# Weights behind the first block's inputs, the second block's inputs in the weights' queue, and three blocks re-slotted

## The chip, the cores and the metric

One Trainium2 chip, of which the kernel uses one core. A core has five engines that run their own instruction streams: PE (TensorE, matrix multiply), DVE (VectorE), ACT (ScalarE), POOL (GpSimd) and SP (SyncE, which here only issues DMAs). The time is device microseconds of one execution; the time of a kernel is the median of several.

## The reference, cut to what matters

```python
# q, k, v, alpha: (4, 8, 768, 48) float32;  B, H, S, D
state = np.zeros((B, H, D, D))
for t in range(S):
    state = alpha[:, :, t, :, None] * state + np.einsum('bhd,bhe->bhde', k[:, :, t], v[:, :, t])
    y[:, :, t] = np.einsum('bhd,bhde->bhe', q[:, :, t], state)
x = y.transpose(0, 2, 1, 3).reshape(B * S, H * D)      # 3072 x 384
out = ((x @ w_a) * (x @ w_b)) @ w_out                  # w_a, w_b: 384 x 1536, w_out: 1536 x 384
```

A gated linear recurrence over 768 tokens for 32 heads, then a bilinear feed-forward over its 3072 output rows.

## The kernel before, in words

The sequence is cut into three stretches of 256 tokens, the batch into two pairs, which makes six blocks (`Chunk`, numbers 0 to 5, two batch rows `u` = 0, 1 and 256 tokens each). Blocks 0 and 1 are the first stretch of the two pairs and start from a zero state, blocks 2 and 3 the second, 4 and 5 the third. What is called the first block below is block 0, the second is block 1.

For each block the recurrence runs as a chain of steps. `ld` loads a (alpha), k, q and v; `L` takes logarithms on ACT and adds neighbours (`l2`); `A` forms running sums with one float32 matmul and exponentials of them on ACT (`beta`, `invb`); `mk`, `mq` multiply k and q with these (DVE); `C` transposes the results on PE (or `T` by a DMA) into `kqT`, copied out of PSUM by DVE or ACT; `D` multiplies queries with keys on PE and masks on DVE (`m`); `dec` brings the decay at each half's end to the partitions it scales, as `dec P` by 32 small matmuls (64 rows in the trace) and two exponentials, as `dec D` by two pairs of DMAs through DRAM (`row<-beta`, then `bl<-row`); `v` casts v to bfloat16 (`vx`); `K` updates the state (`Sm`, then `S`); `S`, `Y` and `G` put together the output `xT` of one `u`, which ACT or DVE copy out of PSUM.

The feed-forward of a block has 512 tokens: 12 slices `f` of w_a and w_b (two groups of three matmuls, 512 wide; ACT copies the first, DVE multiplies it with the second into `prod`), then 4 groups of 12 matmuls with w_out (`ff_o`), each followed by an ACT copy and two stores. `ff f u` is the same slice for one `u` only, 256 wide, so that a block's feed-forward can begin when one `u` is ready. `W lo hi` loads columns of w_a and w_b in eight DMAs, `Wo lo hi` four slices of w_out in one. `warm n` are n matmuls on a constant, `gate_w` and `gate_in` are one-element operations on POOL that wait for a load, or that a load must wait for.

Nothing here is scheduled by a compiler. `START` is a list in the order in which instructions are written out to all engines before block 0's feed-forward. From there `PLAN[c]` says at which of the 28 slots of block c's feed-forward (24 groups of three matmuls, then 4 of `ff_o`) which step of which block is written. A step's last letters name its engine or issuing queue: V = DVE, S = ACT, P = POOL, Y = SP. Each engine runs its instructions in that order and waits where an input is not there.

## Time and profile before

| | us |
|---|---|
| median of 3 runs (243.29 to 245.69) | 244.79 |
| the profiled execution | 244.95 |
| its span, first to last instruction | 243.2 |
| PE busy in the span | 205.0 (84%) |
| first feed-forward matmul of block 0 | 34.79 |
| `ff_o` of block 0 begins | 70.25 |
| `ff_o` of block 1 is over | 125.11 |

The span is what the profile shows; 1.75 us of the profiled execution lie around it. PE is the busiest engine, but its clock has two levels, 1.2 and 2.4 GHz, and the profile gives the granted share (0.50 or 1.00), so equal work may take twice as long in one stretch as in another.

### The profile page before, as it was taken

To read this page: it belongs to the slowest core of one execution; us is meant where nothing else is said; L and a number is where in the kernel's file an instruction comes from. 1 tells how busy PE (TensorE), PEld (TensorE's weight loads), DVE (VectorE), ACT (ScalarE), POOL (GpSimd) and SP (SyncE) were. 2 spreads that over 40 slices of the span, in tenths; PEclk is the share of its full clock that TensorE was granted. 3 is DMA by queue.
4 is the path that set the end of the run, shared out by engine and by line. 5 is a ranking of instruction groups with operands and counts; after the bars stand their busy time and mean duration, and the time that the engine had idled before them with its cause. 6 is when DMAs were issued, how large, how long until landed. Compare 5 with 4: busy or idle time off the path is not lost.

```text
span 243.2 us, 5797 instructions
## 1 busy us (share of the span) xinstructions
PE 205.0 (84%) x2458; PEld 118.8 (49%) x2486; DVE 127.7 (53%) x181; ACT 118.8 (49%) x201; POOL 46.8 (19%) x67
## 2 busy tenths in 40 slices
PE   7866137499999799099999999999999989999992
PEld 7654026345666355035654555545555455554461
DVE  6674213438662286068737894178941785125500
ACT  3820043866574777009437594368832424244420
POOL 8845100000508081081000902000000000000000
PEclk9965558959999999659999999999999999999999
DMA  7999999900185989609947497890087000140023
GB/s 179 247 195 178 158 198 256 214 3 3 35 229 122 321 210 261 129 13 268 182 84 153 107 262 156 165 141 3 2 140 157 12 0 3 32 97 3 0 51 79
DMA packets 45930, 30.69 MB, mean 126 GB/s; under 512 B 36673, under 2 KB 42065, under 8 KB 45905
## 3 DMA queue, kind: packets, MB, share of 16 engines
q1 hardware_dynamic: 39200, 14.21, 31.9%
q0 software_dynamic: 6704, 16.12, 29.2%
q8 instruction: 19, 0.31, 0.6%
q14 instruction: 7, 0.05, 0.1%
HBM read 25.98 MB, written 4.74 MB: 126 GB/s over the span
## 4 chain that ended last, share of the span: by engine, by line
PE 57%; DMA 18%; ACT 7%; issue 7%; SPq 4%; DVE 4%; POOL 1%; POOLq 0%; DVEq 0%; ACTq 0%
PE f L377 16%; PE f L358 15%; PE f L368 15%; DMA v_t<-in_v_dram 9%; DMA bl<-row 4%; SPq L169 3%; DMA k_t<-in_k_dram 3%; PE f L205 2%; DMA row<-beta 2%; PE s L279 2%; PE y L290 2%; PE y L306 1%; PE y L313 1%; ACT L183 1%; ACT vx L190 1%
## 5 line engine op out<-in xcount | busy, mean ns | idle before, releaser
L358 PE MATMUL f<-xT,wa_t 128*128 128x512 bf16 (+1 forms) x211 | 60.7, 381 | 3.5 <-ACT xT L297 1.3
L368 PE MATMUL f<-xT,wb_t 128*128 128x512 bf16 (+1 forms) x217 | 59.8, 377 | 0.8 <-issue 0.3
L377 PE MATMUL f<-wo_t,prod 128*128 128x384 bf16 x288 | 48.3, 326 | 0.0
L377 PEld LDWEIGHTS <-prod 128*128 128x128 bf16 x288 | 28.0, 98 | 19.2 <-issue 0.2
L280 DVE TENSOR_TENSOR m<-s,mask 128x1024 bf16<-128x1024 f32 x24 | 29.3, 1222 | 14.4 <-PE s L279 14.4
L358 PEld LDWEIGHTS <-wa_t 128*128 128x128 bf16 x228 | 21.4, 101 | 25.6 <-issue 6.1
L368 PEld LDWEIGHTS <-wb_t 128*128 128x128 bf16 x228 | 21.4, 100 | 22.6 <-issue 2.5
L379 ACT ACTIVATE ot<-f 128x384 f32<-128x384 f32 x24 | 11.7, 490 | 34.0 <-PE f L377 34.0
L205 PE MATMUL f<-l,ut_f 128*128 128x384 f32 x24 | 11.7, 574 | 4.3 <-DVE l L185 4.3
L297 ACT ACTIVATE xT<-y 128x256 bf16<-128x256 f32 (+1 forms) x18 | 10.3, 574 | 9.5 <-PE y L306 7.7
L279 PE MATMUL s<-kqT 64*64 64x128 bf16 x384 | 12.8, 239 | 1.5 <-DVE kqT L258 1.1
L290 PE MATMUL y<-kqT,Sm 64*64 64x128 bf16 x96 | 7.9, 240 | 6.7 <-POOL Sm L341 6.7
L213 DVE TENSOR_TENSOR QKp<-k_t,invb 128x768 bf16<-128x768 f32 x12 | 11.3, 952 | 2.5 <-DMA k_t<-in_k_dram 2.5
L206 DVE TENSOR_TENSOR le<-f,la 128x384 f32<-128x384 f32 x12 | 6.7, 556 | 10.9 <-PE f L205 10.9
L279 PEld LDWEIGHTS <-kqT 64*64 64x64 bf16 x384 | 8.8, 115 | 7.0 <-issue 4.0
L213 DVE TENSOR_TENSOR QKp<-q_t,beta 128x768 bf16<-128x768 f32 x12 | 11.4, 951 | 0.9 <-DMA q_t<-in_q_dram 0.9
L185 POOL TENSOR_TENSOR l<-la 128x768 f32<-128x768 f32 x3 | 5.4, 1812 | 30.0 <-ACT la L183 30.0
L183 ACT ACTIVATE la<-a_t 128x1536 f32<-128x1536 f32 (+1 forms) x7 | 9.1, 1300 | 3.1 <-DMA a_t<-in_alpha_dram 3.1
L327 PEld LDWEIGHTS <-QKp 64*64 64x64 bf16 x384 | 4.5, 114 | 11.7 <-issue 11.7
L290 PE MATMUL y<-kqT,S 64*64 64x128 bf16 x96 | 8.1, 242 | 2.2 <-DVE tmp L340 1.5
L290 PEld LDWEIGHTS <-Sm 64*64 64x64 bf16 x96 | 6.0, 121 | 6.9 <-POOL Sm L341 6.9
L252 PE MATMUL f<-ident,QKp 128*128 128x128 bf16 x96 | 8.1, 234 | 1.5 <-DVE QKp L213 1.5
(231 smaller groups left out, 278.7 us busy)
## 6 DMA issues: line engine op xcount, KB each, us to landing
out_dram<-ot SPq DMA_DIRECT2D x48, 96.0 KB, 2.2
a_t<-in_alpha_dram POOLq DMA_DIRECT2D x4, 768.0 KB, 9.8
q_t<-in_q_dram POOLq DMA_DIRECT2D x4, 768.0 KB, 7.7
k_t<-in_k_dram POOLq DMA_DIRECT2D x4, 768.0 KB, 11.0
v_t<-in_v_dram POOLq DMA_DIRECT2D x4, 768.0 KB, 8.9
wo_t<-in_moe_w_out_dram POOLq DMA_DIRECT2D x3, 384.0 KB, 14.4
a_t<-in_alpha_dram SPq DMA_DIRECT2D x2, 384.0 KB, 4.2
q_t<-in_q_dram SPq DMA_DIRECT2D x2, 384.0 KB, 5.6
```

The costliest lines, as they stand in the source:

```text
L183: nc.scalar.activation(out=ch.la[:, us].rearrange("p b h r d -> p (b h r d)"), in_=ch.a[:, us].rearrange("p b h r d -> p (b h r d)"), func ...
L205: nc.tensor.matmul(p, lhsT=ut_f32, rhs=ch.l2[:, u].rearrange("p h d -> p (h d)"), start=True, stop=True)
L213: eng.tensor_mul(dst[ch.c % 2][:, u, :, :, :D], src[:, u].rearrange("p h r d -> p r h d"), by[:, u])
L252: nc.tensor.transpose(t[:, j, r, p], src[:, u, r, hp:hp + 2, :].rearrange("s h d -> s (h d)"), ident)
L279: nc.tensor.matmul(s2[g * HC:(g + 1) * HC, r, p, rk, :], lhsT=keysT(ch, u, 2 * h + p, g, r, rk), rhs=queriesT(ch, u, 2 * h + p, g, rs), st ...
L280: nc.vector.tensor_mul(m.rearrange("p r a k s -> p (r a) (k s)"), s2.rearrange("p r a k s -> p (r a) (k s)"), maskn(4))
L290: nc.tensor.matmul(y[rs, g, p, :], lhsT=lhsT, rhs=queriesT(ch, u, p, g, rs), start=(p == 0), stop=False, skip_group_check=True)
L297: nc.scalar.activation(out=o_, in_=i_, func=AF.Copy)
L358: nc.tensor.matmul(ap, lhsT=wa_t[:, kk, f * 128:(f + 1) * 128], rhs=ff_x(ch, us)[:, kk], start=(kk == 0), stop=(kk == KT - 1))
L368: nc.tensor.matmul(bp, lhsT=wb_t[:, kk, f * 128:(f + 1) * 128], rhs=ff_x(ch, us)[:, kk], start=(kk == 0), stop=(kk == KT - 1))
L377: nc.tensor.matmul(op, lhsT=ch.prod[:, f, m * C:(m + 1) * C], rhs=wo_t[:, f, :], start=(f == 0), stop=(f == NFF - 1))
L379: nc.scalar.activation(out=ot, in_=op, func=AF.Copy)
```

## The change

Only the two tables change (and, since they are two lines longer, the numbers of all lines behind them, by 2). At the start, SP loads all eight half-inputs of block 0 (a, a, k, q, v, k, q, v), and nothing for block 1. POOL waits (`gate_w q 1`) for the second q of block 0, then issues all weights, in thirds, with a of block 1 ahead of the last third of w_a and w_b, and v, k, q, q, k, v of block 1 at the end. Fewer `warm` matmuls stand at the very start (18 for 52) and more between the steps of block 0. Block 1's steps stand in the last four slots (24 to 27) of block 0's feed-forward where they were spread over slots 0 to 26, and block 1 gets half-width slices (`ff f u`), as block 0 has. Block 2 takes its decay by matmuls (`dec P`) where it used DMAs (`dec D`), and its loads are written at slots 16 to 25 of block 0.

```diff
 START = [
-    (0, "new"), (0, "ld a 0 Y"), (0, "L 0 V"), (1, "new"), (0, "ld a 1 Y"), (0, "ld q 0 Y"), (1, "gate_in a 0"), (0, "ld k 0 Y"), (0, "ln"),
-    (0, "ld v 0 Y"), (0, "ld k 1 Y"), (0, "warm 52"), (0, "ld q 1 Y"), (0, "ld v 1 Y"), (0, "W 0 512"), (0, "L 1 V"), (0, "exp"), (1, "gate_in k 1"),
-    (0, "W 512 1536"), (1, "ld a * Y"), (0, "Wo 8 12"), (0, "A 0"), (0, "gate_w q 0"), (0, "Wo 0 4"), (0, "warm 22"), (0, "A 1"), (1, "ld q * Y"),
...
+    (0, "new"), (0, "ln"), (0, "ld a 0 Y"), (0, "ld a 1 Y"), (0, "ld k 0 Y"), (0, "L 0 V"), (0, "ld q 0 Y"), (0, "warm 18"), (0, "ld v 0 Y"),
+    (0, "ld k 1 Y"), (0, "ld q 1 Y"), (1, "new"), (0, "ld v 1 Y"), (0, "L 1 P"), (0, "A 0"), (0, "gate_w q 1"), (0, "W 0 512"), (0, "W 512 1024"),
+    (1, "ld a * P"), (0, "exp"), (0, "W 1024 1536"), (0, "Wo 4 8"), (0, "Wo 0 4"), (0, "A 1"), (1, "ld v 0 P"), (0, "Wo 8 12"), (1, "ld k 0 P"),
...
 PLAN = {
-    0: [(0, 1, "L * V"), (6, 1, "A 0"), (8, 1, "A 1"), (8, 1, "mk 0 V"), (9, 1, "mq 0 V"), (10, 1, "mk 1 V"), (11, 1, "dec P"), (14, 1, "mq 1 V"),
...
+    0: [(9, 1, "L * V"), (14, 1, "A 1"), (16, 1, "A 0"), (16, 1, "dec P"), (16, 2, "new"), (16, 2, "ld a * P"), (22, 2, "ld v * P"),
+        (24, 1, "v 0 S"), (25, 1, "mk 0 V"), (25, 2, "ld k * P"), (25, 2, "ld q * P"), (25, 1, "mq 0 V"), (25, 1, "C 0 0 V"), (25, 1, "C 0 1 S"),
...
-    1: [(1, 2, "mq 0 V"), (3, 3, "new"), (4, 3, "ld a * P"), (5, 2, "dec D"), (5, 2, "mq 1 V"), (5, 2, "mk 1 V"), (6, 2, "C 0 0 S"), (6, 2, "v * P"),
...
+    1: [(0, 1, "ff 1 1"), (2, 3, "new"), (5, 1, "ff 3 1"), (5, 3, "ld k * P"), (5, 3, "ld a * P"), (6, 1, "ff 2 1"), (6, 2, "L * V"),
+        (7, 3, "ld q * P"), (10, 1, "ff 0 1"), (10, 2, "A 0"), (10, 2, "A 1"), (11, 2, "mk 0 V"), (12, 2, "dec P"), (12, 3, "ld v * P"),
...
```

Place one, the loads. On SP, before: block 0's eight half-loads, then block 1's four whole ones (tiles a_t, q_t, k_t, v_t; 128x8x96 is a half-load, 128x16x96 a whole one).

```order
L169 DMA a_t<-in_alpha_dram 128x8x96 x2
L169 DMA q_t<-in_q_dram 128x8x96
L169 DMA k_t<-in_k_dram 128x8x96
L169 DMA v_t<-in_v_dram 128x8x96
L169 DMA k_t<-in_k_dram 128x8x96
L169 DMA q_t<-in_q_dram 128x8x96
L169 DMA v_t<-in_v_dram 128x8x96
L169 DMA a_t<-in_alpha_dram 128x16x96
L169 DMA q_t<-in_q_dram 128x16x96
L169 DMA k_t<-in_k_dram 128x16x96
L169 DMA v_t<-in_v_dram 128x16x96
```

After: block 0's alone, k ahead of q, and then the stores of block 0's output and of the first half of block 1's (ot).

```order
L171 DMA a_t<-in_alpha_dram 128x8x96 x2
L171 DMA k_t<-in_k_dram 128x8x96
L171 DMA q_t<-in_q_dram 128x8x96
L171 DMA v_t<-in_v_dram 128x8x96
L171 DMA k_t<-in_k_dram 128x8x96
L171 DMA q_t<-in_q_dram 128x8x96
L171 DMA v_t<-in_v_dram 128x8x96
L387 DMA out_dram<-ot 64x384 x12
```

Block 1's loads have left SP. On POOL, before, from the end of the weights' issue (wo_t; go is the gate's one-element tile; S_103 and tmp belong to the state update; the last two rows are loads of block 2):

```order
L149 DMA wo_t<-in_moe_w_out_dram 128x4x384
L401 COPY go<-q_t 1x1
L149 DMA wo_t<-in_moe_w_out_dram 128x4x384 x2
L341 TENSOR_TENSOR S_103<-tmp,bl_108 128x4x48
L341 TENSOR_TENSOR S_103<-tmp,bl_112 128x8x48
L169 DMA a_t<-in_alpha_dram 128x16x96
L169 DMA q_t<-in_q_dram 128x16x96
```

After, the same place, where the six half-loads at the end are block 1's:

```order
L151 DMA wo_t<-in_moe_w_out_dram 128x4x384 x2
L171 DMA v_t<-in_v_dram 128x8x96
L151 DMA wo_t<-in_moe_w_out_dram 128x4x384
L171 DMA k_t<-in_k_dram 128x8x96
L171 DMA q_t<-in_q_dram 128x8x96 x2
L171 DMA k_t<-in_k_dram 128x8x96
L171 DMA v_t<-in_v_dram 128x8x96
L343 TENSOR_TENSOR S_103<-tmp,bl_108 128x4x48
```

The rest of block 1's loads stand behind w_a, w_b and most of w_out, and the first state update of block 0 on POOL stands behind them.

Place two, the end of block 0's feed-forward on DVE. Before (rows with prod are block 0's products; kqT, Sm_105, tmp, m and xT are steps of block 1):

```order
L258 COPY kqT<-f 128x4x256
L337 TENSOR_TENSOR Sm_105<-s_838,bl_112 128x8x48
L340 TENSOR_TENSOR tmp<-s_838,Sm_105 128x384
L370 TENSOR_TENSOR prod<-as__836,f 128x512
L280 TENSOR_TENSOR m<-s_962,mask 128x1024
L370 TENSOR_TENSOR prod<-as__942,f 128x512
L280 TENSOR_TENSOR m<-s_993,mask 128x1024
L370 TENSOR_TENSOR prod<-as__990,f 128x512
L280 TENSOR_TENSOR m<-s_1027,mask 128x1024
L295 CAST xT<-y_944 128x2x3x128
L370 TENSOR_TENSOR prod<-as__1083,f 128x512
L280 TENSOR_TENSOR m<-s_1141,mask 128x1024
```

After:

```order
L372 TENSOR_TENSOR prod<-as__880,f 128x512
L215 TENSOR_TENSOR QKp_110<-k_t,invb 128x16x48
L215 TENSOR_TENSOR QKp_110<-q_t,beta 128x16x48
L260 COPY kqT<-f 128x4x256
L282 TENSOR_TENSOR m<-s_949,mask 128x1024
L339 TENSOR_TENSOR Sm_105<-y_967,bl_112 128x4x48
L342 TENSOR_TENSOR tmp<-y_967,Sm_105 128x192
L215 TENSOR_TENSOR QKp_110<-k_t,invb 128x16x48
L215 TENSOR_TENSOR QKp_110<-q_t,beta 128x16x48
L282 TENSOR_TENSOR m<-s_1041,mask 128x1024
L260 COPY kqT<-f 128x4x256 x2
L282 TENSOR_TENSOR m<-s_1140,mask 128x1024
```

The products come first, in one row, and block 1's steps from mk (QKp_110<-k_t) on stand behind the last product.

Place three, the decay of block 2 on SP. Before, behind the eight stores of block 0's output (row and bl_108 are block 2's decay):

```order
L385 DMA out_dram<-ot 64x384 x8
L219 DMA row<-beta 2x1x384 x2
L222 DMA bl_108<-row 48x16x1 x2
L262 DMA_TRANSPOSE kqT<-QKp_110 128x16x128
L385 DMA out_dram<-ot 64x384 x4
```

After, from the stores on:

```order
L387 DMA out_dram<-ot 64x384 x12
L264 DMA_TRANSPOSE kqT<-QKp_110 128x16x128
L387 DMA out_dram<-ot 64x384 x4
L221 DMA row<-beta 2x1x384 x2
L224 DMA bl_112<-row 48x16x1 x2
```

Block 2's pair of DMA steps is gone; the first pair left (bl_112) is block 3's.

## Rows read from the trace of the kernel before

**Rows 1.** The page, part 2: granted clock and DMA share in 40 slices of 6.08 us.

```profile
PEclk9965558959999999659999999999999999999999
DMA  7999999900185989609947497890087000140023
```

**Rows 2.** The waits: who waited for whom, total us, times, longest us.

```profile
ACT vx L190 <- DMA v_t<-in_v_dram: 10.7, 1, 10.7
PE y L327 <- ACT xT L297: 9.2, 1, 9.2
...
PE y L290 <- POOL Sm L341: 6.7, 1, 6.7
...
PE f L205 <- DVE l L185: 4.3, 2, 3.9
```

**Rows 3.** The timeline of SP: start us, us, then the issue.

```profile
5.77 1.44 SPq L169 DMA_DIRECT2D k_t<-in_k_dram  x1
...
13.67 19.94 SPq L169 DMA_DIRECT2D q_t<-in_q_dram  x1
```

**Rows 4.** The chain that ended last, in time: start us, us, what.

```profile
8.74 22.95 DMA v_t<-in_v_dram
31.72 0.84 ACT vx L190
...
33.47 0.71 ACT xT L297
...
56.00 0.83 PE s L234 x64
...
92.53 10.28 DMA bl<-row
...
104.81 1.40 PE f L358 x3
...
126.28 0.65 PE f L368 x3
...
148.01 7.80 PE f L377 x48
...
167.81 0.65 PE f L205 x2
...
178.16 7.80 PE f L377 x48
```

**Rows 5.** The timeline of PE: start us, us, line, operation, count [idle before it].

```profile
1.38 5.73 PE L201 MATMUL f<-ident 128*128 128x128 bf16 x52 [1.38 <-POOL ident masks.py:199]
...
12.70 1.07 PE L252 MATMUL f<-ident,QKp 128*128 128x128 bf16 x16 [1.23 <-DVE QKp L213]
...
22.50 1.06 PE L252 MATMUL f<-ident,QKp 128*128 128x128 bf16 x8
...
34.79 0.82 PE L358 MATMUL f<-xT,wa_t 128*128 128x256 bf16 x3
...
44.54 0.49 PE L368 MATMUL f<-xT,wb_t 128*128 128x256 bf16 x3
...
70.25 2.11 PE L377 MATMUL f<-wo_t,prod 128*128 128x384 bf16 x12
...
81.91 0.81 PE L358 MATMUL f<-xT,wa_t 128*128 128x512 bf16 x2 [0.36 <-ACT xT L297]
...
125.11 0.42 PE L279 MATMUL s<-kqT 64*64 64x128 bf16 x16
```

**Rows 6.** Two windows: length; busy PE, PEld, DVE, ACT, POOL; clock, DMA share, GB/s.

```profile
6.00:8.00 2.00, 1.61 (x13) 1.23 (x11) 1.79 (x3) 1.95 (x2) 2.00 (x6) 1.00 1.29 261
28.00:30.00 2.00, 0.00 (x0) 0.00 (x0) 0.00 (x0) 0.00 (x0) 0.00 (x0) 0.50 1.29 166
```

**Rows 7.** The tile wa_t: issue on POOL (ns min/median/max) and time to landing.

```profile
L145 POOL DMA_DIRECT2D wa_t<-in_moe_w_a_dram x4: 602/606/734, 6.7 to 14.9; - x4
...
DMA to landing us min/median/max: 6.5/7.9/10.8
```

**Rows 8.** The page, part 5: busy us, mean ns of one, idle before it.

```profile
L280 DVE TENSOR_TENSOR m<-s,mask 128x1024 bf16<-128x1024 f32 x24 | 29.3, 1222 | 14.4 <-PE s L279 14.4
...
L213 DVE TENSOR_TENSOR QKp<-q_t,beta 128x768 bf16<-128x768 f32 x12 | 11.4, 951 | 0.9 <-DMA q_t<-in_q_dram 0.9
```

46 rows, old and new, of tables (PLAN, START) are left out of this document.

## The prediction

> **What bounds the kernel now.** I read the clock and DMA lines of the page first, then the waits, the chain in order of time, and the timelines of SP and PE at the places that these name. The DMA engines are busy without a break for the first eight slices (48 us), and the clock falls to half in two early stretches and once more near 100 us [rows 1]. In the DMA-bound stretch PE stands still: 9.2 us before the state step L327, released by ACT, whose cast of v had waited 10.7 us for v's second half [rows 2]. That load was issued at 8.74 and took 22.95 us [rows 4], though the issues of the same size ahead of it took 1.44 us each [rows 3]. In between POOL's weights and block 1's loads had joined: SP's next loads crawl (one issue of 19.94 us [rows 3]) and the 261 GB/s of the inputs alone become 166 [rows 6]. So the first half-width feed-forward matmul comes at 34.79 [rows 5].
>
> Two more stops follow. After the half-width slices (the last group starts at 44.54 [rows 5]) the next work on PE is block 1's running sum, 3.9 us late [rows 2], and the clock goes with it [rows 1]. Then block 2's decay comes back through DRAM: 10.28 us for bl<-row, and PE waits 6.7 us before it can read Sm [rows 2, 4], after which three matmuls take 1.40 instead of 0.65 [rows 4]. Behind block 1's output, from 125.11 [rows 5], PE is hardly ever idle: the outputs of blocks 2 and 3 begin at 148.01 and 178.16 [rows 4], 30.15 us apart. That is the steady price of a block: 12 pairs of groups at 2 x 0.65 (15.6), four output groups (7.8), and 6.75 for the recurrence of one block that is transposed by DMA.
>
> **The loads after the change.** Block 0's inputs are 8 x 393 KB = 3.15 MB, alone on the DMA engines. At 261 GB/s [rows 6] from 2 us on they take 12 us: the second q lands near 12.6, the last v near 14. POOL waits for that q and issues the first weights then; with the 2 us or so that an issue needs to start moving data, weights flow from about 14.5. What do they cost? Block 0 and 1 inputs (6.29 MB) at 261 GB/s are 24 of the some 45 us that the DMA engines were busy without a break [rows 1], so the 3.54 MB of bfloat16 weights cost 21, or 7.1 us for each third, wo included. By that w_a and w_b's thirds land near 20, 25 and 34 (4.7 each, block 1's a of 3.0 between the last two), wo near 42, k and q of block 1's first row near 43 and 45, the last v near 49. The sum of the DMA work is unchanged, and so is its end; its order is what changes.
>
> **First feed-forward.** Had v been there, PE's last transposes (22.50 plus 1.06 [rows 5]) would have been followed by ACT's copy (0.9), its xT copy (0.71 [rows 4]) and the state step (0.6): 25.8, so 9.0 us of the 34.79 are v's. From the first transposes at 12.70 [rows 5] that is a chain of 13.1. Off it go 0.9 for the second q, which now is there [rows 8], and 0.7 for the xT copy, which moves to DVE ahead of the transposes. Against it stands the start: the 52 warming matmuls took 5.73 us [rows 5], 0.11 each, the price at 1.2 GHz. 18 of them end at 3.4, and nothing follows until the logarithms near 7.5. I take PE at the low level there: two sums at twice the 0.65 of [rows 4], 24 warming matmuls (2.6), dec P (0.83 [rows 4]): first transposes at 13.5 (12.0 if the clock holds, when DVE's products bound it). Together 13.5 + 13.1 - 1.6 = **25.0**. The weights it needs came near 20.
>
> **Rest of block 0.** Eight half-width pairs at 0.66, the output steps of the second row, and 2 us for a mask and a copy that they wait for: 9.2, against 10.1 in the rows (34.79 to 44.54 plus 0.3 [rows 5]); until 34.2. Eight full pairs at 1.30, block 1's two sums (1.3) and dec P (0.83) are 12.5; ACT must fit two table switches, the logarithm, eight exponentials and eight slice copies in the same stretch, which I price at 1.2: until 47.9 (`ff_o` stood at 70.25 [rows 5]). The stop of 3.9 goes, since a lands near 29 and its logarithm is wanted near 36. Two output groups end at 51.8.
>
> **Block 1's steps, now without cover.** They were spread over the feed-forward; now they stand in the last two output groups and behind them, and PE waits for DVE: mask 1.22 twice and products of 0.95 twice [rows 8] in a row are longer than the output group beside them. PE's own work is the lower bound: two output groups (3.9) and about 6 of steps, 9.9. The upper is what the same chain took in block 0, 13.1. I take 11.4, nearer the lower one because PE is at 2.4 GHz here: 63.2. Half-width slices with the second row's output steps between them: 6.6, until 69.8. This is the price of the change, some 5 us of PE idle that was not there.
>
> **Block 1's feed-forward.** The steady 30.15, less four pairs already done (5.2), plus block 2's transposes on PE and dec P (1.8 + 0.83) and block 3's two sums (1.3), is 28.9. Block 2's whole recurrence now falls on eight slices, not twelve, so ACT and DVE are as full as PE: 3 more (0, and 6 if every chain of block 2 is exposed as block 1's is). Block 1 is over at 101.7, against 125.11 [rows 5]; from its first full slice it used to take 43.2 us (81.91 to 125.11 [rows 5]). The decay's wait of 6.7 and the slow stretch behind it are gone with dec P.
>
> **Behind that** nothing of weight changes: as many steps of blocks 2 to 5, in nearly the same slots, on a PE that was busy anyway. 243.2 - 125.1 = 118.1, plus 0.3 for one D step of block 3 that moves behind the line. Span 220.1; with the 1.75 around it, 221.9 against the profiled 244.95, which is the median (244.79) within 0.1%. **Forecast: 222.0 us.**
>
> **Rivals.** *Late weights.* Before, weights moved from the first issue at 6.7 [rows 7] until about 40, 33 us for 3.54 MB, beside other traffic. If that is POOL's own pace, not sharing, wo lands at 14.5 + 33 + 4.5 (the inputs ahead of it) = 52.0 where I need it at 47.9, and the second q of the first pair comes about 1.5 too late as well: 227.5. Against: input loads on the same engines ran at 261 alone, and the mix at 166 [rows 6].
>
> *POOL is held while it issues.* 34 DMAs now go out on POOL while DVE works. If each waits for one DVE operation of some 0.69 us, the last v lands 23 us later, near 72, where block 1's second state step wants it near 59: 235. Against: the issues took 602 to 734 ns [rows 7] while DVE was busy 1.79 of 2 us [rows 6]. The Trainium skill (SBUF — State Buffer, Summary: rules for kernel authors) tells this way: descriptors of DMAs from GpSimd are starved while VectorE runs in its fast modes, and such DMAs should go out from another queue. By it, moving block 1's inputs to POOL is the wrong way; the durations in the trace do not show it.
>
> *Another wait for a decay.* Block 3's is now the first to go through DRAM, at the end of block 1. If it meets block 4's loads as block 2's met theirs (10.28 [rows 4]), PE waits 6.7 and loses about 2.8 to the low clock: 231.5. Against: block 4's loads are written seven slots and more ahead of it, as before.
>
> *The gate doesn't hold.* If weights still ran beside block 0's inputs, v would be late again and the first slice at 34.8: 231.8.
>
> *Slower: the clock stays low.* Between 25.0 and 101.7 lie 24 pairs and two blocks' outputs. At 1.2 GHz a pair takes 2.80 for 1.30 [rows 4] and an output twice as long: 24 x 1.5 + 15.6 = 52 us lost, 274. It decides from 23 us on, when under half of that work runs at 2.4 GHz. For it: the exposed chains of blocks 0 and 1 are full of short stops, and stops cost the clock before [rows 1]. Against: it came back within a slice each time that work resumed [rows 1], and warming matmuls fill the first chain.
>
> **How the numbers follow.** Forecast 0.66 (216 to 227: first slice 23.5 to 26.5, block 1's chain 9.9 to 13.1, crowding 0 to 6), late weights 0.15, decay 0.10, gate 0.03, POOL held 0.03, low clock 0.03. The range 212 to 234 leaves out the clock, POOL's hold, and the far ends of the others, since several of the terms could be off in the same direction. About 1% is what three runs of this kernel tell from no change (they span 2.4 us). Faster by over 1%: 0.94, all but the clock and combinations of several rivals; within 1%: 0.03; slower: 0.03.
>
> **What would show it.** First half-width slice near 25, not 35; the casts of v without a DMA wait; `ff_o` of block 0 near 48; block 1's output over near 102; no row<-beta before that; PE idle of some 5 us between 52 and 64; the last 118 us as before. Wrong if PE waits on wa_t, wb_t, wo_t or on block 1's k, q or v, or if the clock line shows half behind 30 us.

## The result, and the profile after

The changed kernel took 225.83 us (225.17 to 226.48, 4 runs) where the kernel before took 244.31 (243.29 to 245.69): a ratio of 0.924, with a 95% interval of 0.918 to 0.930. Forecast were 222.0 us and 212 to 234. The profiled execution took 226.01 us, its span 224.2. Medians below are over all executions; ratios leave out those in which the cores of a die ran longer at a lower clock (four of six in the repeat of the changed kernel, three of six with v on POOL, two of four with block 1's loads on SP, whose profile is of one, and one each without the gate and with the early decay).

The page, part 2: granted clock and DMA share in 40 slices, here of 5.6 us.

```profile
PEclk9999999999999988999999999999999999999998
DMA  7999999999999201999489995500782000320022
```

Against [rows 1] all three half-clock stretches are gone; a short one shows near 78 to 90 us (the record of the clock has it from 82.5 to 85.9). Of the stretch ahead of 10.8 us the record says nothing: its first row stands there, and the views print 1.00 where there is none. The DMA engines are busy without a break to 48.6 us in [rows 1] and to about 73 us here, since block 2's loads now follow at once (the first is issued at 41.7, before at 63.8).

The waits (who waited for whom, total us, times, longest us):

```profile
POOL wb_t L148 <- DMA a_t<-in_alpha_dram: 4.6, 1, 4.6
...
PE f L207 <- DVE l L187: 3.6, 1, 3.6
...
PE y L308 <- DVE m L282: 2.8, 3, 1.3
```

The three waits of PE in [rows 2] have no successor of their size; ACT's cast of v no longer waits for a load. The long waits for a load that are left are POOL's (the 4.6 here, and 5.6 at the gate); PE's longest, 3.6 us, is the start, where it waits for the first logarithms.

PE's timeline at the points that the prediction names (start us, us, line, operation, count, idle before it):

```profile
12.53 0.62 PE L254 MATMUL f<-ident,QKp 128*128 128x128 bf16 x8
...
21.96 0.49 PE L360 MATMUL f<-xT,wa_t 128*128 128x256 bf16 x3
...
30.80 0.81 PE L360 MATMUL f<-xT,wa_t 128*128 128x512 bf16 x2
...
44.98 4.06 PE L379 MATMUL f<-wo_t,prod 128*128 128x384 bf16 x24
...
61.10 0.50 PE L360 MATMUL f<-xT,wa_t 128*128 128x256 bf16 x3
...
67.26 0.81 PE L360 MATMUL f<-xT,wa_t 128*128 128x512 bf16 x2
...
102.99 0.81 PE L360 MATMUL f<-xT,wa_t 128*128 128x512 bf16 x2
```

The reader compares with [rows 5]: the first half-width slice came at 34.79 and comes at 21.96, 12.8 us earlier; `ff_o` of block 0 at 70.25 and now 44.98, 25.3 earlier, of which 12.8 are the first slice's and the rest comes of block 1's steps, with the stop of 3.9 among them, no longer standing between; block 1's output was over at 125.11 and is over at 102.99, 22.1 earlier. The span is 19.0 shorter. So 3.1 us of the lead are lost behind block 1. Most of that is at one place: the distance to block 2's output was 148.01 - 125.11 = 22.9 [rows 4, 5], and is now 128.21 - 102.99 = 25.2 (next fence).

The chain that ended last, around block 3's decay (start us, us, what):

```profile
107.27 1.66 DMA row<-beta
...
109.48 2.46 DMA bl<-row
...
112.06 0.57 DVE Sm L343
...
128.21 7.80 PE f L379 x48
...
158.79 7.80 PE f L379 x48
```

This is what [rows 4] showed of block 2's decay, in small: 2.46 us for bl<-row instead of 10.28, and PE idle 1.01 before it can read Sm and 1.20 before a mask's product.

### The profile page after: what moved, and what is told of

It reads as the page before. It is cut to its first block, busy times and chain, and to the rows that moved or that the text cites. A ratio compares the mean times of both kernels' runs of the same rounds, so it can differ in the third digit from the quotient of the medians.

```text
span 224.2 us, 6017 instructions
## 1 busy us (share of the span) xinstructions
PE 199.1 (89%) x2558; PEld 118.2 (53%) x2584; DVE 130.9 (58%) x189; ACT 120.2 (54%) x208; POOL 55.8 (25%) x79
## 4 chain that ended last, share of the span: by engine, by line
PE 74%; DVE 10%; issue 5%; ACT 5%; DMA 2%; POOL 1%; SPq 1%; POOLq 0%; DVEq 0%; ACTq 0%
PE f L379 21%; PE f L360 17%; PE f L370 17%; PE f L207 4%; DVE m L282 3%; PE s L281 3%; PE y L308 3%; PE y L292 2%; PE f L254 2%; PE y L315 1%; DVE kqT L260 1%; PE s L329 1%; DMA bl<-row 1%; PE f L203 1%; DVE mask L135 1%
## 5 line engine op out<-in xcount | busy, mean ns | idle before, releaser
L360 PE MATMUL f<-xT,wa_t 128*128 128x512 bf16 (+1 forms) x229 | 59.1, 358 | 2.6 <-ACT as__760 L364 1.3
L370 PE MATMUL f<-xT,wb_t 128*128 128x512 bf16 (+1 forms) x225 | 58.7, 359 | 2.4 <-ACT as__1368 L364 1.2
L360 PEld LDWEIGHTS <-wa_t 128*128 128x128 bf16 x240 | 22.4, 98 | 22.6 <-issue 2.7
L370 PEld LDWEIGHTS <-wb_t 128*128 128x128 bf16 x240 | 22.1, 98 | 22.4 <-issue 3.1
L381 ACT ACTIVATE ot<-f 128x384 f32<-128x384 f32 x24 | 11.8, 491 | 35.0 <-PE f L379 34.9
L187 POOL TENSOR_TENSOR l<-la 128x768 f32<-128x768 f32 (+1 forms) x3 | 4.6, 1534 | 43.7 <-ACT la L185 43.6
L281 PE MATMUL s<-kqT 64*64 64x128 bf16 x384 | 11.4, 221 | 1.4 <-DVE kqT L260 0.7
L342 DVE TENSOR_TENSOR tmp<-s,S 128x384 f32<-128x384 f32 x4 | 2.2, 558 | 15.9 <-PE s L329 15.9
L281 PEld LDWEIGHTS <-kqT 64*64 64x64 bf16 x384 | 7.7, 105 | 6.0 <-issue 3.9
L308 PE MATMUL y<-m,vx 64*48 64x128 bf16 x384 | 7.6, 217 | 2.8 <-DVE m L282 2.8
L258 ACT ACTIVATE kqT<-f 128x1024 bf16<-128x1024 bf16 x5 | 5.1, 1023 | 8.9 <-PE f L254 8.8
L308 PEld LDWEIGHTS <-vx 64*48 64x48 bf16 x384 | 6.0, 99 | 5.9 <-issue 5.8
L292 PE MATMUL y<-kqT,S 64*64 64x128 bf16 x96 | 7.0, 221 | 2.3 <-DVE tmp L342 1.5
```

The costliest lines, as they stand in the source:

```text
L281: nc.tensor.matmul(s2[g * HC:(g + 1) * HC, r, p, rk, :], lhsT=keysT(ch, u, 2 * h + p, g, r, rk), rhs=queriesT(ch, u, 2 * h + p, g, rs), st ...
L292: nc.tensor.matmul(y[rs, g, p, :], lhsT=lhsT, rhs=queriesT(ch, u, p, g, rs), start=(p == 0), stop=False, skip_group_check=True)
L308: nc.tensor.matmul(ch.y[u][r * DP:r * DP + D, g, p, :], lhsT=ch.vx[g * HC:(g + 1) * HC, u, 2 * p + r, rk, :], rhs=ch.m[u, p // 2][g * HC:( ...
L360: nc.tensor.matmul(ap, lhsT=wa_t[:, kk, f * 128:(f + 1) * 128], rhs=ff_x(ch, us)[:, kk], start=(kk == 0), stop=(kk == KT - 1))
L370: nc.tensor.matmul(bp, lhsT=wb_t[:, kk, f * 128:(f + 1) * 128], rhs=ff_x(ch, us)[:, kk], start=(kk == 0), stop=(kk == KT - 1))
L381: nc.scalar.activation(out=ot, in_=op, func=AF.Copy)
```

## The experiments

All start from the changed kernel unless another is named. Differences between variants of it under some 1.5% can't be told apart by the times (executions of one variant spread over up to 3.3 us), so there the milestones of the profile decide.

**The loads alone.** The order of the kernel before, with the new order and queues of the loads.

```diff
-    (0, "new"), (0, "ld a 0 Y"), (0, "L 0 V"), (1, "new"), (0, "ld a 1 Y"), (0, "ld q 0 Y"), (1, "gate_in a 0"), (0, "ld k 0 Y"), (0, "ln"),
-    (0, "ld v 0 Y"), (0, "ld k 1 Y"), (0, "warm 52"), (0, "ld q 1 Y"), (0, "ld v 1 Y"), (0, "W 0 512"), (0, "L 1 V"), (0, "exp"), (1, "gate_in k 1"),
-    (0, "W 512 1536"), (1, "ld a * Y"), (0, "Wo 8 12"), (0, "A 0"), (0, "gate_w q 0"), (0, "Wo 0 4"), (0, "warm 22"), (0, "A 1"), (1, "ld q * Y"),
-    (0, "dec P"), (1, "ld k * Y"), (0, "warm 4"), (0, "Wo 4 8"), (0, "mq 0 V"), (0, "mk 0 V"), (0, "C 0 0 V"), (0, "C 0 1 S"), (0, "v 0 V"),
-    (0, "D 0 0 s2"), (0, "K 0 V y2"), (1, "ld v * Y"), (0, "mk 1 V"), (0, "S 0"), (0, "D 0 1 s2"), (0, "mq 1 V"), (0, "Y 0 S"), (0, "v 1 S"),
+    (0, "new"), (0, "ld a 0 Y"), (0, "L 0 V"), (1, "new"), (0, "ld a 1 Y"), (0, "ld k 0 Y"), (0, "ld q 0 Y"), (0, "ln"),
+    (0, "ld v 0 Y"), (0, "ld k 1 Y"), (0, "warm 52"), (0, "ld q 1 Y"), (0, "ld v 1 Y"),
+    (0, "gate_w q 1"), (0, "W 0 512"), (0, "W 512 1024"), (1, "ld a * P"), (0, "W 1024 1536"), (0, "Wo 4 8"), (0, "Wo 0 4"), (1, "ld v 0 P"), (0, "Wo 8 12"),
+    (1, "ld k 0 P"), (1, "ld q 0 P"), (1, "ld q 1 P"), (1, "ld k 1 P"), (1, "ld v 1 P"),
+    (0, "L 1 V"), (0, "exp"), (0, "A 0"), (0, "warm 22"), (0, "A 1"),
...
```

> The kernel before with the loads, the gate and the weights of the changed kernel, in its order and on its queues; all other steps of START and all slots of the plan as before (steps of block 1 spread over block 0's slots, no half-width slices for block 1, block 2's decay by DMA). If order alone makes the gain: 226 us. If the slots make it: 244 us. Mine: the first half-width slice comes near 23 as in the changed kernel, but block 1's steps in the middle of block 0's slots then wait for k, q and v that land near 45 to 50, and block 2's decay still waits: 232 to 237 us.

Measured: 240.16 us, ratio 0.989 (0.984 to 0.994). PE's timeline:

```profile
24.75 0.82 PE L360 MATMUL f<-xT,wa_t 128*128 128x256 bf16 x3
...
39.14 1.65 PE L207 MATMUL f<-l,ut_f 128*128 128x384 f32 x2 [3.93 <-DVE l L187]
...
53.32 0.81 PE L360 MATMUL f<-xT,wa_t 128*128 128x512 bf16 x3 [2.73 <-DVE prod L372]
...
77.07 0.81 PE L360 MATMUL f<-xT,wa_t 128*128 128x512 bf16 x2 [0.36 <-ACT xT L299]
...
99.90 0.32 PE L292 MATMUL y<-kqT,Sm 64*64 64x128 bf16 x2 [7.38 <-POOL Sm L343]
```

The first slice is 10.0 us earlier than in [rows 5], as the loads promise. Of that, 4.8 are left at block 1's first full slice (81.91 in [rows 5], 77.07 here): the stop of 3.9 for block 1's running sum has only moved with the rest, though its input lay there from 33.8 on (in these slots it hangs on the order of the steps, not on the load), and block 1's v, now the last load of all, holds ACT for 2.93 and with it PE. At 99.90 the wait for block 2's decay is there again, even longer. The loads alone bring 1.1%. The other half, the new slots on the old loads, was not run.

**The loads, and block 2's decay by matmuls.**

```diff
-    1: [(1, 2, "mq 0 V"), (3, 3, "new"), (4, 3, "ld a * P"), (5, 2, "dec D"), (5, 2, "mq 1 V"), (5, 2, "mk 1 V"), (6, 2, "C 0 0 S"), (6, 2, "v * P"),
+    1: [(1, 2, "mq 0 V"), (3, 3, "new"), (4, 3, "ld a * P"), (5, 2, "dec P"), (5, 2, "mq 1 V"), (5, 2, "mk 1 V"), (6, 2, "C 0 0 S"), (6, 2, "v * P"),
```

> The order of the kernel before, with the new order of the loads, and block 2's decay by matmuls in place of DMAs (same slot). With the loads alone it took 240.2, with PE waiting 7.4 for block 2's Sm at 99.9 and three slices at half clock behind it. If that wait ate the gain of the loads, it is gone here: 240.2 - 7.4 - 2.0 (clock) + 0.8 (64 small matmuls) = 231.6, range 230 to 234, and block 2's outputs begin some 8 us earlier. Rival: the old slots, with block 1's steps waiting for block 1's own loads (a, then v), set the time and the decay only stood in their shadow: 238 to 240.

Measured: 231.56 us, ratio 0.949 (0.945 to 0.953), as expected. By the ratios the step from "dec D" to "dec P" is worth 4.0%, some 9.7 us (8.6 by the medians, which were taken on two chips), and the output of block 2 begins at 134.07 instead of 142.89, 8.8 earlier. The wait for one small transfer, with the half-clock stretch behind it, cost nearly what the loads had gained at the first slice.

**Block 2's decay back to DMAs, in the changed kernel.**

```diff
-        (7, 3, "ld q * P"), (10, 1, "ff 0 1"), (10, 2, "A 0"), (10, 2, "A 1"), (11, 2, "mk 0 V"), (12, 2, "dec P"), (12, 3, "ld v * P"),
+        (7, 3, "ld q * P"), (10, 1, "ff 0 1"), (10, 2, "A 0"), (10, 2, "A 1"), (11, 2, "mk 0 V"), (12, 2, "dec D"), (12, 3, "ld v * P"),
```

> The changed kernel with block 2's decay through DRAM again (dec D for dec P in slot 12 of block 1), as before. If dec P itself took the stop of 6.7 us and the slow clock behind it away: those 9 us come back, 235 us. Mine: in the changed kernel no load is on its way between 75 and 89 us, so the two DMA steps take some 2 us each, end ahead of the state step that wants them, and PE is spared 0.8 us of small matmuls: 225 to 226 us. That would say that it was the meeting with the loads, not the way through DRAM, that cost the time.

Measured: 226.00 us, ratio 0.930 (0.924 to 0.937); its profile's span is 223.7. No difference that can be told. SP's timeline:

```profile
75.90 1.32 SPq L221 DMA_DIRECT2D row<-beta  x2
78.45 0.92 SPq L224 DMA_DIRECT2D bl<-row  x2
```

The same transfers, in a lull of the DMA engines (2, 0 and 1 tenths from 73 to 90 us in the line above), hold nobody: the second bl<-row has landed at 81.1, 2.7 us after the first was issued, and the state update that reads it starts at 84.2. So it was not the way through DRAM that cost 9 to 10 us, but the moment, with 3.1 us to spare where 10.28 would not have fitted: with the slots placed anew the decay could have stayed as it was.

**Without the gate.** `gate_w q 1` left out, so that POOL issues weights from 7.96 on.

```diff
-    (0, "ld k 1 Y"), (0, "ld q 1 Y"), (1, "new"), (0, "ld v 1 Y"), (0, "L 1 P"), (0, "A 0"), (0, "gate_w q 1"), (0, "W 0 512"), (0, "W 512 1024"),
+    (0, "ld k 1 Y"), (0, "ld q 1 Y"), (1, "new"), (0, "ld v 1 Y"), (0, "L 1 P"), (0, "A 0"), (0, "W 0 512"), (0, "W 512 1024"),
```

> The changed kernel with only the gate taken out, so that POOL issues the weights some 5 us earlier, beside block 0's k, q and v; every byte and every other step as in the changed kernel. Order theory (the weights' packets beside block 0's inputs are what made v late): the second half of v lands well after 20 us instead of near 15, the first half-width slice comes near 32 instead of 21.96, and about 8 to 10 us are lost: 234 us. Rival (the gain comes from the new slots, and earlier weights only help): 225 to 226 us.

Measured: 231.74 us, ratio 0.951 (0.944 to 0.958): the gate is worth 2.7%, but not by the way that was expected. ACT's timeline, and then PE's:

```profile
22.44 0.84 ACT L192 ACTIVATE vx<-v_t 128x768 bf16<-128x768 f32 x1 [7.30 <-DMA v_t<-in_v_dram]
```

```profile
19.33 0.36 PE L281 MATMUL s<-kqT 64*64 64x128 bf16 x12 [2.15 <-issue]
...
24.34 0.50 PE L360 MATMUL f<-xT,wa_t 128*128 128x256 bf16 x3
...
117.39 0.31 PE L292 MATMUL y<-kqT,Sm 64*64 64x128 bf16 x2 [3.56 <-DVE Sm L343]
```

v waits again, but lands at 22.4, not at 31.7 as in [rows 4], because POOL itself stood for 4.9 us in seven stops between its issues (each until an earlier weight DMA had landed), and block 1's loads are not on SP. But it is not v that makes the first slice 2.4 late. PE had already lost 2.15 us from 17.18 on, in the middle of a group of like matmuls and with nothing to wait for ("issue"), and all that follows comes 2.4 later at the changed kernel's distances; v's cast was over at 23.28, and the state step that needs it began at 23.96, 0.55 behind the transposes ahead of it, as in the changed kernel. By itself v would have held that step by at most 1.8 (an estimate: 23.28 against 21.48 in the changed kernel).

What PE stood for is a reading, not an experiment. The trace holds packets of 16 KB that carry instructions (the page, part 3, has 20 of them on its queue q8). One is on its way here from 16.46 to 17.85, and PE goes on 1.48 behind its end; in the changed kernel one took from 13.95 to 15.10, and PE did not stand. So PE's own instructions seem to have come late beside weights and inputs.

Of the lead lost, 2.2 us are still left at block 1's last two output groups (101.25, against 99.09). The other 2.4 of the 4.6 by which its span is longer come later, at block 3's decay. The chain there:

```profile
112.01 4.12 DMA bl<-row
```

Where it took 2.46 in the changed kernel it takes 4.12, and PE waits 3.56 for Sm. This belongs to coming 2 us late, not to the gate: the repeat of the changed kernel below, whose profiled execution is 2.15 late at block 1's last two output groups for another reason (half clock from 61.1 to 64.5), shows 4.27 for bl<-row and the same 3.56 on PE. What makes the transfer longer there was not tried.

**Block 1's loads on SP.** They follow block 0's there and run beside the weights.

```diff
-    (1, "ld a * P"), (0, "exp"), (0, "W 1024 1536"), (0, "Wo 4 8"), (0, "Wo 0 4"), (0, "A 1"), (1, "ld v 0 P"), (0, "Wo 8 12"), (1, "ld k 0 P"),
-    (1, "ld q 0 P"), (1, "ld q 1 P"), (0, "warm 24"), (1, "ld k 1 P"), (1, "ld v 1 P"), (0, "mk 0 V"), (0, "dec P"), (0, "v 0 S"), (0, "mq 0 V"),
+    (1, "ld a * Y"), (0, "exp"), (0, "W 1024 1536"), (0, "Wo 4 8"), (0, "Wo 0 4"), (0, "A 1"), (1, "ld v 0 Y"), (0, "Wo 8 12"), (1, "ld k 0 Y"),
+    (1, "ld q 0 Y"), (1, "ld q 1 Y"), (0, "warm 24"), (1, "ld k 1 Y"), (1, "ld v 1 Y"), (0, "mk 0 V"), (0, "dec P"), (0, "v 0 S"), (0, "mq 0 V"),
```

> The changed kernel with block 1's loads issued on SP behind block 0's, where nothing holds them, instead of on POOL between and behind the weights. Order theory: they now run beside the weights and take their turns, so the first third of the weights lands near 26 instead of 20 and the later thirds and wo later too, while block 1's inputs come earlier than they are needed: PE waits 4 to 6 us, 230 to 232 us. Rival (the DMA engines do the same sum of work, and which queue issues it does not matter): 226 us. A third, the skill's rule that POOL's issue is starved beside VectorE: faster than the changed kernel, 223 us or less.

Measured: 234.66 us, ratio 0.956 (0.947 to 0.966). The tile wa_t, time from issue to landing, first here and then in the changed kernel:

```profile
DMA to landing us min/median/max: 6.6/7.4/8.1
```

```profile
DMA to landing us min/median/max: 3.0/4.2/8.6
```

The weights take 7.4 us where they took 4.2, and the first slice comes at 27.68, 5.7 late. But PE waits for no weight here. It stands twice ahead of that slice, both times in the middle of a group of like matmuls and with no releaser, 4.9 us together:

```profile
19.61 0.36 PE L281 MATMUL s<-kqT 64*64 64x128 bf16 x12 [2.13 <-issue]
...
27.45 0.24 PE L329 MATMUL y<-vx,QKp 64*64 64x48 bf16 x4 [2.77 <-issue]
```

The first stop is at PE's 449th instruction, the same one as without the gate, the second 256 instructions on. The packets of instructions take from 16.92 to 18.11 and from 24.54 to 25.83, where the changed kernel has them at 13.95 to 15.10 and 19.32 to 20.22; PE goes on 1.50 and 1.62 behind their ends. The granted clock is 1.00 in the record from 11.8 to 28.9, so neither stop is the clock's doing. So moving the loads cost 3.2% by the ratios, some 7.9 us, and at the first slice the loss is in these stops. That they come of the loads beside them is read from two runs that agree, and was not tried by itself. What the slower weights would have cost can't be told from this run.

**Without the warming matmuls between the steps** (24, 6, 8, 14 and 18 of them left out).

```diff
-    (1, "ld q 0 P"), (1, "ld q 1 P"), (0, "warm 24"), (1, "ld k 1 P"), (1, "ld v 1 P"), (0, "mk 0 V"), (0, "dec P"), (0, "v 0 S"), (0, "mq 0 V"),
-    (0, "C 0 0 V"), (0, "warm 6"), (0, "C 0 1 S"), (0, "D 0 0 s2"), (0, "K 0 P y2"), (0, "warm 8"), (0, "warm 14"), (0, "v 1 S"), (0, "S 0"),
-    (0, "mk 1 V"), (0, "D 0 1 s2"), (0, "mq 1 V"), (0, "warm 18"), (0, "Y 0 V"), (0, "C 1 0 V"), (0, "G 0 V"), (0, "D 1 0 s2"), (0, "C 1 1 S"),
+    (1, "ld q 0 P"), (1, "ld q 1 P"), (1, "ld k 1 P"), (1, "ld v 1 P"), (0, "mk 0 V"), (0, "dec P"), (0, "v 0 S"), (0, "mq 0 V"),
+    (0, "C 0 0 V"), (0, "C 0 1 S"), (0, "D 0 0 s2"), (0, "K 0 P y2"), (0, "v 1 S"), (0, "S 0"),
+    (0, "mk 1 V"), (0, "D 0 1 s2"), (0, "mq 1 V"), (0, "Y 0 V"), (0, "C 1 0 V"), (0, "G 0 V"), (0, "D 1 0 s2"), (0, "C 1 1 S"),
```

> The changed kernel without the 70 warming matmuls between block 0's steps (24, 6, 8, 14 and 18); the 18 at the start stay. If they hold the clock: the granted clock shows half from about 10 to 25 us, the transposes, sums and half-width slices take twice as long there, and 2 to 4 us are lost: 228 to 230 us. Rival (PE waits for DVE there anyway, so that nothing is lost but idle time): 225.5 to 226.5 us.

Measured: 229.52 us, ratio 0.943 (0.938 to 0.948). PE's timeline:

```profile
19.24 1.05 PE L308 MATMUL y<-m,vx 64*48 64x128 bf16 x32 [1.33 <-DVE m L282]
20.23 1.04 PE L254 MATMUL f<-ident,QKp 128*128 128x128 bf16 x8
...
24.16 0.60 PE L360 MATMUL f<-xT,wa_t 128*128 128x256 bf16 x3
```

And a window of it (length; busy PE, PEld, DVE, ACT, POOL; clock, DMA share, GB/s):

```profile
20.00:24.00 4.00, 3.86 (x82) 3.04 (x73) 3.18 (x5) 0.31 (x1) 3.63 (x6) 1.00 1.18 180
```

The same y<-m,vx took 0.63 in the changed kernel, the same transposes 0.70 and 0.62. PE ran its chain at the lower level: 1.04 for eight such transposes is the 1.06 of [rows 5], from a half-clock stretch. The 1.00 in the window is no record of the clock: in this run its first row stands at 24.39 us, and the views print 1.00 where there is none. First slice 2.2 late: the 70 small matmuls pay for themselves before the feed-forward begins.

**Block 3's decay earlier**, from slot 27 to 24 of block 1's feed-forward, and so ahead of its transposing DMAs on SP.

```diff
-        (21, 3, "mk 0 V"), (22, 3, "A 1"), (22, 2, "S 1"), (22, 2, "D 1 1 s2"), (23, 3, "mk 1 V"), (24, 2, "Y 1 S"), (25, 2, "G 1 S"),
-        (25, 3, "mq 0 V"), (25, 3, "T 0 Y"), (26, 3, "mq 1 V"), (27, 3, "dec D"), (27, 3, "T 1 Y"), (27, 4, "ld a * P")],
+        (21, 3, "mk 0 V"), (22, 3, "A 1"), (22, 2, "S 1"), (22, 2, "D 1 1 s2"), (23, 3, "mk 1 V"), (24, 2, "Y 1 S"), (24, 3, "dec D"), (25, 2, "G 1 S"),
+        (25, 3, "mq 0 V"), (25, 3, "T 0 Y"), (26, 3, "mq 1 V"), (27, 3, "T 1 Y"), (27, 4, "ld a * P")],
```

> The changed kernel with block 3's decay (by DMA) written in slot 24 of block 1 instead of slot 27. In the changed kernel its first DMA stands on SP behind the stores of block 1's output, is issued at 106.5 though its input is there at 95.9, and its result lands at 111.9, where DVE and then PE wait for it (2.4 us idle on PE, and more behind). Theory: it is SP's order; issued behind the first store, it lands ahead of need, 2.5 to 3.5 us gained: 222.5 to 223.5 us. Rival (the wait is DVE's full list, the DMA only ends last by a little; DVE waited 0.7 us for it): 225 to 226 us.

Measured: 228.48 us, ratio 0.938 (0.933 to 0.943); a gain is excluded. SP's timeline, and then PE's:

```profile
98.51 1.31 SPq L221 DMA_DIRECT2D row<-beta  x2
103.42 0.91 SPq L224 DMA_DIRECT2D bl<-row  x2
...
105.71 2.12 SPq L264 DMA_TRANSPOSE kqT<-QKp  x1
```

```profile
110.22 0.42 PE L281 MATMUL s<-kqT 64*64 64x128 bf16 x16 [2.02 <-DMA kqT<-QKp]
```

SP, having issued row<-beta, stands from 99.82 until 103.42 for its return, and the transposing DMA behind it goes out 4.95 later than in the changed kernel (105.71 for 100.76). PE now waits 2.02 for kqT and 0.46 for Sm. The wait has changed its name.

**Block 3's decay by matmuls.**

```diff
-        (25, 3, "mq 0 V"), (25, 3, "T 0 Y"), (26, 3, "mq 1 V"), (27, 3, "dec D"), (27, 3, "T 1 Y"), (27, 4, "ld a * P")],
+        (25, 3, "mq 0 V"), (25, 3, "T 0 Y"), (26, 3, "mq 1 V"), (27, 3, "dec P"), (27, 3, "T 1 Y"), (27, 4, "ld a * P")],
```

> The changed kernel with block 3's decay by matmuls in place of DMAs. PE stood about 2.2 us in all between 110.9 and 116.4 behind a row<-beta that SP could issue only at 106.5, behind block 1's stores, and a bl that landed at 111.9. My theory: that is the last wait for a decay; without it 2.2 less 0.8 for the small matmuls: 224.4 by the run of 225.8 (1.0 to 1.8 below the repeat of the changed kernel beside it), with no idle over 0.5 us on PE in front of the y matmuls of block 3. Rival: PE waits as long for the masks and for S next (DVE is full there) and pays the matmuls on top: 226 to 227.

Measured: 228.97 us, ratio 0.936 (0.931 to 0.940), span 224.5 in the profile: no gain. At its place the expected happened; further on stands another wait. PE's timeline:

```profile
112.69 0.24 PE L292 MATMUL y<-kqT,Sm 64*64 64x128 bf16 x2 [0.34 <-DVE Sm L343]
...
126.79 7.96 PE L379 MATMUL f<-wo_t,prod 128*128 128x384 bf16 x48
...
140.39 0.81 PE L370 MATMUL f<-xT,wb_t 128*128 128x512 bf16 x3 [1.64 <-DVE prod L372]
```

And DVE's, just ahead of the last of these:

```profile
139.18 0.56 DVE L343 TENSOR_TENSOR Sm<-tmp,bl 128x384 bf16<-128x384 f32 x1 [2.51 <-DMA bl<-row]
```

Block 2's output begins 1.3 us earlier (126.79 for 128.05 in the same view of the changed kernel). Then DVE stands 2.51 in front of block 4's Sm, whose decay also goes through DRAM, a product queues behind it, and PE loses 1.64. In the changed kernel DVE came to the same instruction at 138.10 and found the decay there. With block 4's decay by matmuls too, the lead might hold; that was not tried.

**Block 3's logarithm later**, from slot 15 to 19 of block 1's feed-forward, its sum on DVE.

```diff
-        (15, 3, "L * P"), (16, 2, "D 0 0 s2"), (16, 2, "K * P"), (17, 2, "C 1 1 S"), (18, 2, "S 0"), (18, 4, "new"), (18, 2, "D 0 1 s2"),
+        (16, 2, "D 0 0 s2"), (16, 2, "K * P"), (17, 2, "C 1 1 S"), (18, 2, "S 0"), (18, 4, "new"), (18, 2, "D 0 1 s2"), (19, 3, "L * V"),
```

> The changed kernel with block 3's logarithm and neighbour sum written at slot 19 of block 1 (and the sum on DVE) where they stood at slot 15. ACT worked without a break from 67.1 to 83.1, and the last piece of that was this logarithm (2.8 us with its table load); PE stood 1.33 at 82.4 and the clock was at half until 85.5. If ACT's load in that stretch is what block 1's feed-forward pays for, its output is over 1.5 to 2.5 us earlier (about 101 for 103.0), the clock stays at full level, and the time is 224 (1.5 to 2 below the repeat). Rival: the work only moves to where block 2's xT copies and the exponentials of block 3 stand; 226 to 228 and a stop of PE near 90 instead.

Measured: 228.23 us, ratio 0.936 (0.932 to 0.939). Two windows of it (columns as above):

```profile
79.00:82.00 3.00, 1.40 (x35) 0.61 (x36) 2.70 (x4) 0.95 (x2) 0.00 (x0) 1.00 0.00 0
82.00:86.00 4.00, 4.00 (x78) 2.14 (x75) 1.71 (x3) 1.02 (x1) 1.91 (x3) 0.57 0.01 4
```

And PE's timeline:

```profile
81.89 0.78 PE L329 MATMUL s<-vx,QKp 64*64 64x48 bf16 x64 [1.33 <-DVE m L282]
90.55 0.91 PE L207 MATMUL f<-l,ut_f 128*128 128x384 f32 x2 [1.48 <-DVE l L187]
```

ACT is free (0.95 busy of 3, it was 2.97), and the stop of 1.33 and the low clock are there all the same. My theory, ACT's load, falls. Another stop of 1.48 has come to it.

**Block 2's cast of v on POOL**, instead of ACT.

```diff
-        (12, 2, "mq 0 V"), (13, 2, "mk 1 V"), (13, 2, "mq 1 V"), (14, 2, "C 0 0 V"), (14, 2, "v * S"), (15, 2, "C 0 1 S"), (15, 2, "C 1 0 V"),
+        (12, 2, "mq 0 V"), (13, 2, "mk 1 V"), (13, 2, "mq 1 V"), (14, 2, "C 0 0 V"), (14, 2, "v * P"), (15, 2, "C 0 1 S"), (15, 2, "C 1 0 V"),
```

> The changed kernel with block 2's cast of v on POOL, idle there, instead of ACT. In the changed kernel ACT works without a break from 67.5 to 83 us, and the cast (1.48 us) stands ahead of the copy of the transposes that PE's next slice and the next mask wait for. If ACT's list sets the pace in block 1's crowded slots: 1 to 1.5 us gained, 224.5 us. If DVE's does (its products end only 0.4 us ahead of that copy): no change within 0.5 us.

Measured: 228.63 us, ratio 0.928 (0.922 to 0.934); not told from the changed kernel. Its profile has the best span of all, 223.3, with the stop in front of block 2's K there (1.53) and the clock behind it held.

**Both, the earlier decay of block 3 and v on POOL** (the diffs of these two together).

> Both of the last two together: block 3's decay in slot 24 and block 2's cast of v on POOL. If the two losses are separate, the gains add: 221.5 to 222.5 us. If one hides the other, no better than the better of the two.

Measured: 227.25 us, ratio 0.932 (0.928 to 0.936). PE waits 1.86 for the transposing DMA, as with the early decay alone.

**The changed kernel once more**, beside the last three.

> The changed kernel once more, on the chip of these three: the measure for differences of one per cent. 225.8, between 225 and 228; milestones within 0.7 of the first profile (first half-width slice 22.0, output of block 0 begins 45.0, first half-width slice of block 1 61.1, output of block 1 over 103.0).

Measured: ratio 0.926 (0.920 to 0.931), from executions of 225.60 and 226.31 us. None of the six variants of its slots is shown to beat it; the early decay, the decay by matmuls and the later logarithm are 1.0 to 1.5% slower by the ratios, close to what can be told.

## Why the prediction was right, point by point

The forecast was 3.8 us too low, by terms that erred to both sides. By the steps of the prediction, with the measured pieces from the timeline of PE above:

| step | predicted us | measured us |
|---|---|---|
| first half-width slice | 25.0 | 21.96 |
| half-width slices of block 0 | 9.2 | 8.84 |
| to `ff_o` of block 0 | 13.7 | 14.18 |
| two output groups and block 1's chain | 15.3 | 16.12 |
| block 1's half-width slices | 6.6 | 6.16 |
| to the end of block 1's output | 31.9 | 35.73 |
| the rest | 118.4 | 121.21 |
| span | 220.1 | 224.2 |

**The loads** went as worked out in their order, somewhat late: the gate at 13.54 for 12.6, block 1's a at 32.8 for 29 (ACT's logarithm starts then, and PE stands 1.34 us at 36.2 in its wake), the last v of block 1 at 52.3 for 49. POOL's timeline:

```profile
13.54 0.18 POOL L403 COPY go<-q_t 1x1 f32<-1x1 f32 x1 [5.63 <-DMA q_t<-in_q_dram]
13.66 0.74 POOL L147 DMA_DIRECT2D wa_t<-in_moe_w_a_dram  x1
...
33.08 0.53 POOL L148 DMA_DIRECT2D wb_t<-in_moe_w_b_dram  x1 [4.57 <-DMA a_t<-in_alpha_dram]
```

**First slice, 3.0 too late in the forecast.** The chain from the first transposes was taken from the kernel before, where PE ran it at half clock in part: 11.5 us after subtractions. It took 9.43 (12.53 to 21.96). The experiment without warming matmuls shows the other price, 12.6 (11.53 to 24.16). The transposes themselves came 1.0 early: the two sums took the low-level price that I had put in (2.7 for 2.6), but the first of them began at 7.04 for 7.5, and the 24 warming matmuls took 2.0 for 2.6.

**Block 1's feed-forward, 3.8 too short.** This is the term that was mis-sized most: "3 more" for crowding (0 to 6) came out at 5.1 to 5.6. Windows of the changed kernel (length; busy PE, PEld, DVE, ACT, POOL; clock, DMA share, GB/s):

```profile
67.00:73.00 6.00, 4.68 (x23) 2.47 (x23) 3.19 (x6) 5.71 (x8) 0.00 (x0) 1.00 1.03 260
73.00:79.00 6.00, 5.55 (x98) 3.20 (x97) 5.22 (x7) 5.96 (x14) 0.00 (x0) 1.00 0.24 61
79.00:82.00 3.00, 1.55 (x23) 0.78 (x24) 2.85 (x5) 2.97 (x3) 0.00 (x0) 1.00 0.00 0
82.00:86.00 4.00, 3.25 (x76) 2.44 (x77) 1.54 (x4) 1.44 (x3) 2.59 (x2) 0.57 0.02 4
86.00:103.00 17.00, 16.80 (x225) 10.05 (x226) 11.46 (x14) 9.93 (x19) 6.87 (x6) 1.00 0.89 216
```

PE is idle for 1.3, 0.5, 1.5, 0.8 and 0.2 us, 4.2 in all, and its 3.25 at a clock of 0.57 are work for some 1.9 at the full one, which loses 1.4 (an estimate; the early-decay run has the same groups at the full level in 0.9 less, 5.60 for 6.47). Together 5.1 to 5.6; the remaining 1.2 to 1.7 are PE work that my sum of 28.9 missed. DVE is nearly full from 73 to 82 (8.07 of 9): block 2's products, copies and first mask. The experiment with the later logarithm took ACT out of that stretch and left the stop as it was, so what is left is DVE's row of block 2's steps, of which PE waits for the mask at 82.41; no experiment took that row out, so this is argued and not shown.

**The rest, 2.8 too short,** is the rival that I named "another wait for a decay" and gave 0.10, in part: not 6.7 and 2.8 but 2.2 of idle before block 2's output, and 0.4 more between the outputs of blocks 2 and 3 (158.79 - 128.21 = 30.6, for 30.15 [rows 4]). The decay stood behind a transposing DMA and block 1's stores on SP, and did not meet block 4's loads, as the rival had it.

**The other rivals.** Late weights: no wait of PE for wa_t, wb_t or wo_t. The argument against it was weaker than it looked, though: nearly alone on the DMA engines, from 17 to 39 us, the weights still moved at 132 to 189 GB/s by the page, so the 166 of [rows 6] is not the price of the mix. POOL held: its issues of weights still took 0.53 to 0.74 us each, with DVE working beside them, and no wait of PE came of them. The rule of the Trainium skill that the prediction weighed there (SBUF — State Buffer, Summary: rules for kernel authors) does not show in this kernel; moving block 1's loads off POOL, as it would have it, made the kernel slower. No row shows in which mode a VectorE operation ran, so this says nothing of the rule elsewhere. The gate held; without it the place lost 2.4, and by PE's stop, not the 9.8 of the rival by v. Its 231.8 us fits the measured 231.74 by accident, since half of the loss came at block 3's decay. By its record, which begins at 10.8 us, the clock stayed high but for 82 to 86.

**The signs.** Most came as named: the first slice, the casts of v, block 1's output over near 102, no row<-beta ahead of that. Two did not. PE is idle for 2.1 us between 52 and 64 (9.89 of 12 busy), not some 5; the prediction's own terms, 11.4 against 9.9 of work, left only 1.5. And the clock shows half behind 30 us, from 82.5 to 85.9, which it had named as a sign of being wrong; that stretch is in the loss of block 1's feed-forward above.

**What the gain consists of.** By the ratios the loads alone bring 1.1%, block 2's decay by matmuls 4.0 more, and the new slots with the warming matmuls 2.5 more. But the second step is not a gain of "dec P" as such, since in the new slots "dec D" does as well. The prediction read the loads, the chain and the decay as one sum; the runs show that in the old slots the loads are worth little. In the new slots their order is worth 2.7% (the gate) and 3.2% (the queue). What the new slots are worth on the old loads stays open.

## What to carry to other kernels

When loads are put in the order of their use, place the steps anew as well, or the gain runs into the next wait that stood in the old one's shadow: 10.0 us at the first slice were 1.1% (2.7 us) at the end. A transfer of a few KB through DRAM was free in a lull and cost 9 to 10 us under load: look at what the DMA engines do in that microsecond, and at what stands behind it in its queue, before replacing it. Removing one wait of 1 or 2 us from a chain with several such transfers bought nothing here, because the next one took it up. And a stop of PE without a releaser, in the middle of a group of like matmuls, need not be a wait for data: look past the load that is late beside it.

## What the runs showed of the hardware that was not expected

POOL stood with eight of its DMAs under way. In the changed kernel, a load of block 1's a, issued at 23.36, took until 33; seven weight DMAs went out behind it, and the eighth stood 4.57 us until it had landed. Without the gate the ninth weight DMA stood from 12.6 until the first had landed, and with block 1's loads on SP from 18.3 to 20.6. In the traces POOL's DMAs use eight semaphores in turn, and each issue waits for the DMA eight before it, whose semaphore it uses again. So this is a wait in this program's instructions; a limit of the engine is not shown by it. No wait of PE is traced to this stop here, though v, k and q of block 1 are issued behind it.

The record of the granted clock does not begin with the span. Its first row stands at 7.05 us in the kernel before, at 10.84 in the changed one and at 24.39 without the warming matmuls; up to there the views show 1.00, while a group that takes 0.63 us elsewhere took 1.05. Ahead of the first row the durations of like groups are the witness.

PE can stand for its own instructions, as it seems: three stops of 2.1 to 2.8 us, two of them at the same instruction in two runs, each 1.5 to 1.6 behind the end of a 16 KB packet of instructions that came later than in the changed kernel. No run tried this alone.

DVE waits beside POOL. The state's S at 113.32 took 1.85 us instead of 0.56, while POOL's sum of logarithms ran from 112.95 (DVE's and POOL's timelines of the changed kernel):

```profile
113.32 1.85 DVE L343 TENSOR_TENSOR S<-tmp,bl 128x384 bf16<-128x384 f32 x1
```

```profile
112.95 1.80 POOL L187 TENSOR_TENSOR l<-la 128x768 f32<-128x768 f32 x1 [20.06 <-ACT la L185]
```

It ends at 115.17, 0.42 after POOL's operation, which fits a wait for that end; the 0.42 left are less than the 0.56 that the operation takes alone, and times on POOL are rough. The Trainium skill has this (SBUF — State Buffer, SBUF: two separate sides): one of the two holds a shared pair of ports for a whole instruction. The trace agrees in this place; a variant whose S came 0.31 ahead of POOL's sum (block 3's decay by matmuls) has its 0.56. Two more runs agree: S took 1.57 with block 2's decay by DMA and 2.00 with v on POOL, and ended 0.41 to 0.42 behind POOL's sum.

The clock's fall at 82 us hangs on more than the order of instructions: the kernel with block 3's earlier decay has the same instructions up to that point, the same stop of 1.33, and a clock line without a dip.
